# Splitting a weight conversion into four steps and moving a row sum by one iteration, in a fused attention and feed-forward kernel

## The chip, the cores and the metric

The kernel runs on one core of a Trainium2 chip. The metric is device time in microseconds (us), the median of three executions. The engines are named as the profile names them: PE (matmuls; its weight loads have a row of their own, PEld), DVE, ACT, POOL, and SP, which only issues DMAs here. Each engine works off its own instructions in order.

## The reference

Two blocks run one after the other. The first is a linear attention with decay over 4 batches, 8 heads, 768 positions and 48 channels per head. The state of each head is multiplied by `w` at every position and takes up the outer product of `k` and `v`; the position's own term is weighted by `u` instead:

```
cur = einsum('bhd,bhe->bhde', u * k_t, v_t)
y_t = einsum('bhd,bhde->bhe', r_t, state + cur)
state = w * state + einsum('bhd,bhe->bhde', k_t, v_t)
```

The second block takes the 3072 rows of 384 values, multiplies them by `w_in` (384 x 1024), computes `h * softmax(h)`, normalises each row to mean 0 and variance 1, scales the 1024 columns by `g_ln` and multiplies by `w_out` (1024 x 384). `w_in` and `w_out` arrive as 64-bit floats.

## The kernel before

The 3072 rows are 24 units of 128 rows (6 chunks of 4 batches). A loop over i from -2 on is a software pipeline written out by hand: in iteration i, unit i+4 is loaded, unit i+2 is transposed and gets its diagonal, unit i+1 gets its scores, unit i is finished (y and state), unit i-2 goes through the first matmul and the softmax, unit i-5 through the second matmul. The order in the program text is the order on each engine; nothing reorders it.

For a unit u the names are: `turn_r` (PE transposes `tr_ps`, DVE writes `rT`, L640), `decay_k` (POOL writes `kp`, L618), `turn_k` (PE `tk_ps`, ACT writes `kT`), `weigh_own` (two multiplications `rku` by POOL, or by DVE for units 0 to 2, L624 and L625; then DVE sums over the channels into `own`, L627), `diagonal` (8 ACT instructions write `AT`, L633, scaled by `own`), `scores` (PE `at`, DVE copies the upper triangle into `AT`, L661), `finish` (PE `y_ps` and `kv_ps`, ACT copies `xT`, DVE adds to `state`, L705 or L708, POOL decays it, L706), `ffn_in` (PE `h_ps`, L716; DVE row maximum `st`, L720; ACT `e`, L722), `unit` (DVE `solu`, L732; ACT square sum `sq`, L736; POOL `st`, L737 and L739), `normalise` (DVE, L744), `turn_ln` (PE `t_ps`, L754; DVE and ACT copy `lnT`, L756 and L758), `ffn_out` (PE `o_ps`, L765; ACT copies `o`, L768; SP stores it).

`h_ps` has one buffer: the first matmul of the next unit can't start before `solu` of this unit has read it. The pool `psM` has four buffers for `tr_ps`, `tk_ps`, the two halves of `t_ps`, `o_ps`, `y_ps` and `kv_ps`, taken in turn, so that the second half of `t_ps` takes the buffer of the last `kv_ps`.

The weights come in 14 pieces (0 to 5 of `w_in`, 128 x 512; 6 to 13 of `w_out`, 128 x 384), each loaded as raw words and converted in iterations -2 to 4 (1, 1, 2, 2, 3, 3, 2 pieces): ACT takes the magnitude (`mag`, L503); DVE clamps it, shifts it and puts the sign back (L504, L508, L510, writing `ma`); ACT scales the low word (`low`, L513); POOL adds both (L515 or L517); for `w_out` ACT scales the sum by `g_ln` (L518). All of a piece is emitted before the next piece:

```
for _ in range(conversions.get(i, 0)):
    convert(todo.pop(0))
    if ahead < len(pieces):
        load_weights(ahead)
        ahead += 1
```

Of the kernel before, what the change touches and what calls it, by code (L numbers as in the profile page):

```python
# [9 lines left out]
F32 = mybir.dt.float32  # L10
U32 = mybir.dt.uint32
ACT = mybir.ActivationFunctionType
ALU = mybir.AluOpType
AX = mybir.AxisListType
# [4 lines left out]
def general_path(  # L19
# [59 lines left out]
    def load(i):  # L79
        b, c = units[i]  # L80
        for t, src in ((kpads, k), (rpads, r), (vts, v)):
            nc.sync.dma_start(out=t[i % NLD][:, :, 0:D],
                              in_=src[b, :, ts(c, T), :].rearrange("h s d -> s h d"))
# [169 lines left out]
    def scores(i):  # L253
        X = live[i]
        AT = X["AT"] = ATs[i % NAT]
        A4 = AT.rearrange("p (a q) t -> p a q t", q=2)
        for ls in LEVELS:
            pss = [psA.tile([128, 2, HP, 64], F32, tag="at", name=f"at{q}") for q in range(2)]
            for n, L in enumerate(ls):
                lo, up = (X["kT"], X["rT"]) if L == 1 else (X["z"][L], X["z"][L])  # L260
                M = 64 if L == 64 else 128
                for a in range(HP):
                    for q in range(2):
                        rows = slice(q * P, q * P + D)
                        rhs = up[rows, a, :].rearrange("p (j o n) -> p j o n", o=2, n=L)[:, :, 1, :]
                        nc.tensor.matmul(pss[q][0:M, n, a, :], lo[rows, a, 0:M], rhs,
                                         start=True, stop=True)
            for n, L in enumerate(ls):
                for q in range(2):
                    dst = halves(A4[:, :, q, :], L)[1]  # L270
                    src = pss[q][:, n].rearrange("p a (j n) -> p a j n", n=L)
                    if L in masks:
                        m = masks[L].rearrange("p o (j n) -> p o j n", n=L)
                        nc.vector.copy_predicated(
                            dst, m.to_broadcast([128, HP, 64 // L, L]), src)
                    else:
                        for j in range(64 // L):
                            rows = slice(2 * L * j, 2 * L * j + L)
                            nc.scalar.copy(out=dst[rows, :, j, :], in_=src[rows, :, j, :])
# [89 lines left out]

    N = len(units)  # L370
    todo = list(range(len(pieces)))
    ahead = 6
    prepare(0)
    for i in range(N + LAG):
        j = i - LAG
        if i + 2 < N:
            load(i + 2)
        if i + 1 < N:
            prepare(i + 1)
# [6 lines left out]
        if j >= 0:  # L386
            ffn_in(j)
        if i < N:
            scores(i)
        if j >= 0:  # L390
            ffn_out(j)
        if i < N:
            finish(i)
# [3 lines left out]
def direct_path(  # L397
# [19 lines left out]
    nc = tc.nc  # L417
    B, H, S, D = r.shape
# [9 lines left out]
    LA, LO = 2, 3  # L428
# [5 lines left out]
    apool = ctx.enter_context(tc.tile_pool(name="apool", bufs=2))  # L434
    fpool = ctx.enter_context(tc.tile_pool(name="fpool", bufs=2))
    wpool = ctx.enter_context(tc.tile_pool(name="wpool", bufs=2))
# [17 lines left out]
    def load(i, which="krv"):  # L454
        b, c = units[i]
        for t, src, n in ((kpads, k, "k"), (rpads, r, "r"), (vts, v, "v")):
            if n in which:
                nc.sync.dma_start(out=t[i % len(t)][:, :, 0:D],
                                  in_=src[b, :, ts(c, T), :].rearrange("h s d -> s h d"))
# [4 lines left out]
    g_sb = const.tile([128, KF], F32, name="g_sb")  # L464
# [7 lines left out]
                        in_=u.rearrange("h d -> (h d)").partition_broadcast(128))  # L472
# [4 lines left out]
    def words(x):  # L477
# [5 lines left out]
    pieces = [(w_in_sb[:, c, ts(n, NX)], w_in_w[ts(c, 128), ts(n, 2 * NX)], None)  # L483
              for n in range(dff // NX) for c in range(KD)]
# [5 lines left out]
        raws[j] = wpool.tile([128, dst.shape[1], 2], U32, tag="raw", name="raw", bufs=5)  # L490
        nc.sync.dma_start(out=raws[j].rearrange("p n o -> p (n o)"), in_=src)

    def convert(j):
        dst, _, f = pieces[j]
        n = dst.shape[1]
        raw = raws.pop(j)
        lo, hi = raw[:, :, 0], raw[:, :, 1]
        mag = wpool.tile([128, n], F32, tag="mag", name="mag")
        ma = wpool.tile([128, n], U32, tag="ma", name="ma")
        low = wpool.tile([128, n], U32, tag="low", name="low")  # L500


        nc.scalar.activation(out=mag, in_=hi.bitcast(F32), func=ACT.Abs)  # L503
        nc.vector.tensor_scalar(out=mag, in0=mag, scalar1=FLOOR, scalar2=CEIL,  # L504
                                op0=ALU.max, op1=ALU.min)


        nc.vector.tensor_scalar(out=ma, in0=mag.bitcast(U32), scalar1=3, scalar2=0x3FFFFFF8,  # L508
                                op0=ALU.logical_shift_left, op1=ALU.bitwise_and)
        nc.vector.scalar_tensor_tensor(out=ma, in0=hi, scalar=0xC0000000, in1=ma,  # L510
                                       op0=ALU.bitwise_and, op1=ALU.bitwise_or)

        nc.scalar.activation(out=low, in_=lo, func=ACT.Copy, scale=2.0 ** -29)  # L513
        if f is None:
            nc.gpsimd.tensor_tensor(out=dst.bitcast(U32), in0=ma, in1=low, op=ALU.add)  # L515
        else:
            nc.gpsimd.tensor_tensor(out=ma, in0=ma, in1=low, op=ALU.add)  # L517
            nc.scalar.activation(out=dst, in_=ma.bitcast(F32), func=ACT.Copy,  # L518
                                 scale=g_sb[:, f : f + 1])

# [65 lines left out]
    def make_wt():  # L586

        nc.gpsimd.memset(wt, 0.0)
        for q in range(2):
            rows = slice(q * P, q * P + D)  # L590
            nc.gpsimd.tensor_copy(out=wt[rows, :, q, :],
                                  in_=pw[rows, 0, 7].unsqueeze(2).to_broadcast([D, HP, D]))
# [16 lines left out]
    live = {}  # L609
# [5 lines left out]
    def decay_k(i):  # L615
        X = live[i] = {}
        X["kp"] = apool.tile([128, H, P], F32, name="kp", bufs=4)
        nc.gpsimd.tensor_mul(X["kp"].rearrange("p h d -> p (h d)"),  # L618
                             kpads[i % NLD].rearrange("p h d -> p (h d)"),
                             kdec.rearrange("p a d -> p (a d)"))  # L620

    def weigh_own(i, engine):
        rku = apool.tile([128, H, D], F32, name="rku")
        engine.tensor_mul(rku, kpads[i % NLD][:, :, 0:D], u_bc)  # L624
        engine.tensor_mul(rku, rku, rpads[i % NLD][:, :, 0:D])  # L625
        own = live[i]["own"] = small.tile([128, H, 1], F32, name="own")
        nc.vector.tensor_reduce(out=own[:, :, 0], in_=rku, axis=AX.X, op=ALU.add)  # L627

    def diagonal(i):
        X = live[i]  # L630
# [4 lines left out]
    def turn_r(i):  # L635
        rT = live[i]["rT"] = apool.tile([128, HP, T], F32, name="rT", bufs=3)
        ps = psM.tile([128, HP, T], F32, tag="m", name="tr_ps")
        for a in range(HP):
            nc.tensor.transpose(ps[:, a, :], pair(rpads[i % NLD], a), ident)
        nc.vector.tensor_mul(rT, ps, fore)  # L640
# [129 lines left out]


    N = len(units)
    todo = list(range(len(pieces)))
    ahead = 5
    conversions = {-2: 1, -1: 1, 0: 2, 1: 2, 2: 3, 3: 3, 4: 2}
    decay_k(0)
    for i in range(-2, N + LA + LO):
        j, l = i - LA, i - LA - LO
        drain = i >= N + LA - 1
        if 0 <= i and i + 4 < N:  # L780
            load(i + 4)
        if i + 2 < N:
            turn_r(i + 2)
            if i <= 0:
                weigh_own(i + 2, nc.vector)
            turn_k(i + 2)
        if i + 3 < N:
            decay_k(i + 3)
        if i == -2:
            make_wt()  # L790
        for _ in range(conversions.get(i, 0)):
            convert(todo.pop(0))
            if ahead < len(pieces):
                load_weights(ahead)
                ahead += 1
        if i + 2 < N:
            diagonal(i + 2)
        if i == 0:
            nc.sync.dma_start(out=g_sb, in_=moe_g_ln.rearrange("(c p) -> p c", p=128))
        if i == 10:  # L800
            check_range()
        if 0 <= l and not (drain and i > N + LA - 1):
            turn_ln(l)
        if 0 <= j < N:
            ffn_in(j)
        if 0 <= i + 1 < N:
            scores(i + 1)
        if 0 <= j < N:
            unit(j)
        if 0 <= i and i + 3 < N:  # L810
            weigh_own(i + 3, nc.gpsimd)
        if drain and l + 1 < N:
            turn_ln(l + 1)
        if 0 <= l:
            ffn_out(l)
        if 0 <= j < N:
            normalise(j)
        if 0 <= i < N:
            finish(i)
# [43 lines left out]
```

## Time and profile before

| what | value |
|---|---|
| time, median of 3 | 455.01 us (453.76 to 455.08) |
| the profiled execution's own time | 454.42 us |
| its span, first to last instruction | 452.7 us |
| busy: PE, PEld | 399.3 us (88%), 248.9 us (55%) |
| busy: DVE, ACT, POOL | 207.5 us (46%), 183.2 us (40%), 125.4 us (28%) |
| mean granted PE clock | 0.946 |
| DMA moved in all | 25.92 MB, mean 57 GB/s |

The profile comes from one execution. Its own time is a little below the median of the runs. A share of busy time is a mean over the whole span, and the start of this kernel, in which weights are loaded and converted, differs from the rest; so the views are read stage by stage.

### The profile page before, as it was taken

The numbers are of one execution on the slowest core, as the hardware profiler recorded it, in microseconds if no ns is written. First come the engines' busy times: TensorE is split into PE (matmuls) and PEld (weight loads), VectorE is DVE, ScalarE is ACT, GpSimd is POOL, SyncE is SP. The second block draws the span as 40 slices with busy tenths as digits, with TensorE's granted clock in tenths as the row PEclk, the third lists the DMA queues.
The fourth block names the chain that finished last, engine by engine and source line by source line (L and its number), as shares of the span: only waits on it lengthen the run. The fifth ranks groups of instructions, "written<-read, shape, count | busy, mean of one in ns | idle before, by whom it ended". The sixth has DMA issues, their size and how long they took to land.

```text
span 452.7 us, 7184 instructions
## 1 busy us (share of the span) xinstructions
PE 399.3 (88%) x2853; PEld 248.9 (55%) x2853; DVE 207.5 (46%) x395; ACT 183.2 (40%) x422; POOL 125.4 (28%) x163
## 2 busy tenths in 40 slices
PE   2598081829999999999999999999999999999995
PEld 2485041325665665675665665666566565655563
DVE  6976454544435345454353443534525433523410
ACT  1872626264434434434343452443443443322320
POOL 4565141414421421421431342242142120000000
PEclk9879677677999999999999999999999999999999
DMA  9999660000303311330330330230330000000011
GB/s 183 261 237 159 152 91 17 1 0 1 71 20 52 70 43 29 70 63 9 70 71 1 70 72 15 57 71 19 52 71 19 0 19 20 19 1 17 17 38 41
DMA packets 81592, 25.92 MB, mean 57 GB/s; under 512 B 76557, under 2 KB 79758, under 8 KB 81550
## 3 DMA queue, kind: packets, MB, share of 16 engines
q1 hardware_dynamic: 81406, 25.18, 27.6%
q8 instruction: 24, 0.39, 0.4%
q10 hardware_dynamic: 144, 0.20, 0.1%
q14 instruction: 18, 0.15, 0.1%
HBM read 20.65 MB, written 4.72 MB: 56 GB/s over the span
## 4 chain that ended last, share of the span: by engine, by line
PE 46%; DVE 25%; POOL 12%; ACT 9%; issue 6%; DMA 1%; POOLq 0%; ACTq 0%; DVEq 0%
PE h_ps L716 24%; PE o_ps L765 13%; DVE solu L732 5%; PE t_ps L754 4%; ACT e L722 4%; POOL rku L625 4%; POOL rku L624 4%; DVE st L720 4%; DVE solu L744 3%; DVE own L627 2%; PE y_ps L686 2%; POOL st L739 2%; ACT sq L736 2%; POOL ma L517 2%; DVE ma L510 2%
## 5 line engine op out<-in xcount | busy, mean ns | idle before, releaser
L716 PE MATMUL h_ps<-w_in_sb,xT 128*128 128x512 f32 x288 | 134.5, 618 | 25.6 <-DVE solu L732 25.2
L765 PE MATMUL o_ps<-w_out_sb,lnT 128*128 128x384 f32 x384 | 129.5, 491 | 0.0
L716 PEld LDWEIGHTS h_ps<-w_in_sb,xT 128*128 128x128 f32 x288 | 55.3, 199 | 87.9 <-issue 86.7
L765 PEld LDWEIGHTS o_ps<-w_out_sb,lnT 128*128 128x128 f32 x384 | 71.2, 190 | 47.9 <-issue 1.0
L720 DVE TENSOR_REDUCE st<-h_ps 128x1 f32<-128x1024 f32 x24 | 29.4, 1224 | 92.0 <-PE h_ps L716 92.0
L737 POOL TENSOR_SCALAR st<-st 128x1 f32<-128x1 f32 x24 | 4.6, 190 | 233.3 <-ACT sq L736 233.3
L722 ACT ACTIVATE e<-h_ps,st 128x1024 f32<-128x1024 f32 x24 | 26.7, 1111 | 95.3 <-DVE st L720 95.3
L633 ACT ACTIVATE AT<-ident,own 128x128 f32<-128x128 f32 x192 | 58.7, 389 | 5.2 <-DVE own L627 5.2
L627 DVE TENSOR_REDUCE own<-rku 128x8 f32<-128x384 f32 x24 | 13.3, 553 | 86.8 <-POOL rku L625 86.6
L736 ACT ACTIVATE sq<-solu,st 128x1024 f32<-128x1024 f32 x24 | 27.6, 1149 | 47.8 <-DVE st L734 47.8
L754 PE MATMUL t_ps<-ident,solu 128*128 128x128 f32 x192 | 29.3, 284 | 9.5 <-ACT xT L698 8.1
L658 PEld LDWEIGHTS at<-rT,kT 48*128 48x128 f32 x384 | 25.7, 198 | 19.8 <-issue 19.0
L658 PE MATMUL at<-rT,kT 48*128 48x128 f32 x384 | 30.6, 298 | 2.7 <-DVE AT L661 2.6
L618 POOL TENSOR_TENSOR kp<-kpad,kdec 128x512 f32<-128x512 f32 x24 | 31.2, 1302 | 6.4 <-ACT kdec L568 5.3
L661 DVE COPY_PREDICATED AT<-later,at 128x512 f32<-128x512 uint32 x48 | 32.0, 722 | 0.0
L732 DVE SCALAR_TENSOR_TENSOR solu<-h_ps,st,e 128x1024 f32<-128x1024 f32 x24 | 30.8, 1284 | 0.8
L754 PEld LDWEIGHTS t_ps<-ident,solu 128*128 128x128 f32 x192 | 22.1, 145 | 15.3 <-ACT xT L698 8.3
L686 PE MATMUL y_ps<-AT,vt 128*32 128x128 f32 x768 | 26.3, 279 | 0.0
L744 DVE TENSOR_SCALAR solu<-solu,st 128x1024 f32<-128x1024 f32 x24 | 20.3, 845 | 10.8 <-POOL st L739 10.8
L648 ACT COPY kT<-tk_ps 128x512 f32<-128x512 f32 x24 | 14.0, 583 | 26.6 <-PE tk_ps L647 26.6
L706 POOL TENSOR_TENSOR state<-state,wt 128x384 f32<-128x384 f32 x16 | 16.0, 1002 | 29.7 <-DVE state L705 29.7
L702 PE MATMUL kv_ps<-vt,kp 128*128 128x96 f32 x160 | 23.5, 292 | 0.0
(67 smaller groups left out, 368.4 us busy)
## 6 DMA issues: line engine op xcount, KB each, us to landing
kpad<-in_k_dram SPq DMA_DIRECT2D x24, 192.0 KB, 3.4
rpad<-in_r_dram SPq DMA_DIRECT2D x24, 192.0 KB, 4.0
vt<-in_v_dram SPq DMA_DIRECT2D x24, 192.0 KB, 3.9
out_dram<-o SPq DMA_DIRECT2D x24, 192.0 KB, 2.0
raw<-in_moe_w_in_dram SPq DMA_DIRECT2D x6, 512.0 KB, 5.8
raw<-in_moe_w_out_dram SPq DMA_DIRECT2D x8, 384.0 KB, 3.4
u_bc<-in_u_dram ACTq DMA_DIRECT2D x1, 192.0 KB, 3.5
wq<-in_w_dram SPq DMA_DIRECT2D x1, 1.5 KB
```

The source lines that it names most:

```text
L633: nc.scalar.activation(out=AT[:, h, :], in_=ident, func=ACT.Copy, scale=X["own"][:, h])
L658: nc.tensor.matmul(pss[q][:, a, :], X["kT"][rows, a, :], X["rT"][rows, a, :], start=True, stop=True)
L661: nc.vector.copy_predicated(A4[:, :, q, :], later.to_broadcast([128, HP, T]), pss[q])
L686: nc.tensor.matmul(y_ps[32 * g : 32 * g + 32, j, :], lhsT, rhs, start=(g not in opened), stop=stop, skip_group_check=True)
L716: nc.tensor.matmul(h_ps[:, ts(n, NX)], X["xT"][:, j, :], w_in_sb[:, j, ts(n, NX)], start=(j == 0), stop=(j == KD - 1))
L720: nc.vector.tensor_reduce(out=nmax, in_=h_ps, axis=AX.X, op=ALU.max, negate=True)
L722: nc.scalar.activation(out=e, in_=h_ps, func=ACT.Exp, bias=nmax, accum_out=se)
L732: nc.vector.scalar_tensor_tensor(out=solu, in0=h_ps, scalar=rs, in1=e, op0=ALU.mult, op1=ALU.mult, accum_out=tot)
L736: nc.scalar.activation(out=sq, in_=solu, func=ACT.Square, bias=nmu, accum_out=ss)
L744: nc.vector.tensor_scalar(out=X["solu"], in0=X["solu"], scalar1=nmu, scalar2=rstd, op0=ALU.add, op1=ALU.mult)
L754: nc.tensor.transpose(t_ps[:, f, :], X["solu"][:, ts(4 * g + f, 128)], ident)
L765: nc.tensor.matmul(o_ps, X["lnT"][:, f, :], w_out_sb[:, f, :], start=(f == 0), stop=(f == KF - 1))
```

## The change

`convert` is cut into four steps. Step a holds both ACT readings of the raw words (`mag` and `low`), step b the three DVE instructions, step c the addition on POOL, step d the scaling by `g_ln` on ACT. In an iteration, a and b of all its pieces come first, then the diagonal, then `decay_k`, then c of all its pieces; d follows in the next iteration, ahead of that one's a. `mag` and `low` get three buffers and `ma` four (two each before). `weigh_own` is cut in two: the multiplications (`weigh`) for unit i+3 stand behind the c steps of iteration i, ahead of the POOL instructions of `unit`, and run on POOL for all units but the first; the sum (`sum_own`) stands one iteration later, behind `turn_r`. `decay_k` moves behind the diagonal, `make_wt` from iteration -2 to -1, and the load of `g_ln` ahead of the loads of unit 4. The diff without the renamed and unchanged lines:

```diff
-    def convert(j):
+    def convert_a(j):
         raw = raws.pop(j)
+        n = raw.shape[1]
         lo, hi = raw[:, :, 0], raw[:, :, 1]
+        mag = wpool.tile([128, n], F32, tag="mag", name="mag", bufs=3)
+        low = wpool.tile([128, n], U32, tag="low", name="low", bufs=3)
         nc.scalar.activation(out=mag, in_=hi.bitcast(F32), func=ACT.Abs)
+        nc.scalar.activation(out=low, in_=lo, func=ACT.Copy, scale=2.0 ** -29)
+        step[j] = hi, mag, low
+    def convert_b(j):
+        hi, mag, low = step[j]
+        ma = wpool.tile([128, mag.shape[1]], U32, tag="ma", name="ma", bufs=4)
...
+        step[j] = ma, low
+    def convert_c(j):
+        dst, _, f = pieces[j]
+        ma, low = step[j]
+        nc.gpsimd.tensor_tensor(out=dst.bitcast(U32) if f is None else ma, in0=ma, in1=low,
+                                op=ALU.add)
+    def convert_d(j):
+        dst, _, f = pieces[j]
+        ma, low = step.pop(j)
+        if f is not None:
             nc.scalar.activation(out=dst, in_=ma.bitcast(F32), func=ACT.Copy,
                                  scale=g_sb[:, f : f + 1])
-    def weigh_own(i, engine):
-        rku = apool.tile([128, H, D], F32, name="rku")
+    def weigh(i, engine):
+        rku = live[i]["rku"] = apool.tile([128, H, D], F32, name="rku")
         engine.tensor_mul(rku, kpads[i % NLD][:, :, 0:D], u_bc)
         engine.tensor_mul(rku, rku, rpads[i % NLD][:, :, 0:D])
+
+    def sum_own(i):
         own = live[i]["own"] = small.tile([128, H, 1], F32, name="own")
-        nc.vector.tensor_reduce(out=own[:, :, 0], in_=rku, axis=AX.X, op=ALU.add)
+        nc.vector.tensor_reduce(out=own[:, :, 0], in_=live[i]["rku"], axis=AX.X, op=ALU.add)
...
+        if i == 0:
+            nc.sync.dma_start(out=g_sb, in_=moe_g_ln.rearrange("(c p) -> p c", p=128))
         if 0 <= i and i + 4 < N:
             load(i + 4)
         if i + 2 < N:
             turn_r(i + 2)
-            if i <= 0:
-                weigh_own(i + 2, nc.vector)
+            if i == -2:
+                weigh(0, nc.vector)
+            sum_own(i + 2)
             turn_k(i + 2)
-        if i + 3 < N:
-            decay_k(i + 3)
-        if i == -2:
-            make_wt()
-        for _ in range(conversions.get(i, 0)):
-            convert(todo.pop(0))
+        for p in now:
+            convert_d(p)
+        now = [todo.pop(0) for _ in range(conversions.get(i, 0))]
+        for p in now:
+            convert_a(p)
+            convert_b(p)
             if ahead < len(pieces):
                 load_weights(ahead)
                 ahead += 1
         if i + 2 < N:
             diagonal(i + 2)
-        if i == 0:
-            nc.sync.dma_start(out=g_sb, in_=moe_g_ln.rearrange("(c p) -> p c", p=128))
+        if i + 3 < N:
+            decay_k(i + 3)
+        for p in now:
+            convert_c(p)
+        if i + 3 < N:
+            weigh(i + 3, nc.gpsimd)
+        if i == -1:
+            make_wt()
...
-        if 0 <= i and i + 3 < N:
-            weigh_own(i + 3, nc.gpsimd)
```

## Rows read from the trace of the kernel before

**Rows 1.** Page part 2: busy tenths of PE and DMA in 40 slices.
```profile
PE   2598081829999999999999999999999999999995
...
DMA  9999660000303311330330330230330000000011
```

**Rows 2.** Waits, whole span: engine, line, releaser; us in total, times, longest us.
```profile
PE h_ps L716 <- DVE solu L732: 25.2, 2, 14.1
...
ACT w_out_sb L518 <- POOL ma L517: 31.6, 8, 7.9
...
PE t_ps L754 <- ACT xT L698: 8.1, 1, 8.1
...
PEld t_ps L754 <- DVE state L705: 5.0, 15, 0.3
```

**Rows 3.** Timeline, 56 to 100 us: start, duration, engine, line, operands [idle before, releaser].
```profile
56.95 1.28 DVE L732 SCALAR_TENSOR_TENSOR solu<-h_ps,st,e 128x1024 f32<-128x1024 f32 x1
...
60.06 0.56 POOL L739 TENSOR_TENSOR st<-st,neg_half 128x1 f32<-128x1 f32 x1
...
60.44 0.55 ACT L503 ACTIVATE mag<-raw 128x384 f32<-128x384 f32 x1
...
63.16 1.27 DVE L744 TENSOR_SCALAR solu<-solu,st 128x1024 f32<-128x1024 f32 x1
...
65.42 0.34 DVE L504 TENSOR_SCALAR mag<-mag 128x384 f32<-128x384 f32 x1
...
70.51 0.99 POOL L517 TENSOR_TENSOR ma<-ma,low 128x384 uint32<-128x384 uint32 x1 [2.62 <-DVE ma L510]
71.54 0.61 ACT L518 ACTIVATE w_out_sb<-ma,g_sb 128x384 f32<-128x384 f32 x1 [2.08 <-POOL ma L517]
...
72.62 0.36 DVE L504 TENSOR_SCALAR mag<-mag 128x384 f32<-128x384 f32 x1 [2.25 <-ACT mag L503]
...
73.95 1.22 DVE L720 TENSOR_REDUCE st<-h_ps 128x1 f32<-128x1024 f32 x1
...
78.09 1.09 ACT L722 ACTIVATE e<-h_ps,st 128x1024 f32<-128x1024 f32 x1
...
79.69 1.28 DVE L732 SCALAR_TENSOR_TENSOR solu<-h_ps,st,e 128x1024 f32<-128x1024 f32 x1
...
81.13 8.10 PE L716 MATMUL h_ps<-w_in_sb,xT 128*128 128x512 f32 x12 [11.17 <-DVE solu L732]
...
98.75 1.28 DVE L732 SCALAR_TENSOR_TENSOR solu<-h_ps,st,e 128x1024 f32<-128x1024 f32 x1
```

**Rows 4.** Timeline: DVE's sum for unit 4.
```profile
41.16 0.55 DVE L627 TENSOR_REDUCE own<-rku 128x8 f32<-128x384 f32 x1 [2.20 <-POOL rku L625]
```

**Rows 5.** Groups by line: operation and count | busy us, mean ns | idle before.
```profile
L624 POOL TENSOR_TENSOR rku<-kpad,u_bc 128x384 f32<-128x384 f32 x21 | 21.2, 1009 | 0.0
```

**Rows 6.** Timeline: a DVE shift beside a POOL addition.
```profile
35.35 1.32 POOL L515 TENSOR_TENSOR w_in_sb<-ma,low 128x512 uint32<-128x512 uint32 x1 [2.09 <-DVE ma L510]
...
35.57 1.38 DVE L508 TENSOR_SCALAR ma<-mag 128x512 uint32<-128x512 uint32 x1
```

**Rows 7.** Timeline, 168 to 178 us: one iteration of the long even stretch.
```profile
168.54 0.55 DVE L627 TENSOR_REDUCE own<-rku 128x8 f32<-128x384 f32 x1 [4.34 <-POOL rku L625]
...
169.73 0.55 DVE L705 TENSOR_TENSOR state<-kv_ps,state 128x384 f32<-128x384 f32 x1
...
170.31 2.44 ACT L633 ACTIVATE AT<-ident,own 128x128 f32<-128x128 f32 x8
170.34 0.42 PEld L754 LDWEIGHTS t_ps<-ident,solu 128*128 128x128 f32 x4 [0.35 <-DVE state L705]
...
177.17 4.81 PEld L765 LDWEIGHTS o_ps<-w_out_sb,lnT 128*128 128x128 f32 x16
```

**Rows 8.** Windows: busy us of PE, PEld, DVE, ACT, POOL; PE clock; DMA share, GB/s.
```profile
39.00:41.00 2.00, 1.85 (x16) 1.09 (x18) 0.00 (x0) 0.00 (x0) 1.92 (x3) 1.00 0.94 262
102.00:107.00 5.00, 5.00 (x12) 3.09 (x13) 2.45 (x5) 2.28 (x8) 3.07 (x4) 0.50 0.00 0
```

More of the change, by code (lines that the diff above doesn't have):

```diff
@@ L491, in load_weights @@
         nc.sync.dma_start(out=raws[j].rearrange("p n o -> p (n o)"), in_=src)
-    def convert(j):
-        dst, _, f = pieces[j]
-        n = dst.shape[1]
+    step = {}
+    def convert_a(j):
         raw = raws.pop(j)
+        n = raw.shape[1]
         lo, hi = raw[:, :, 0], raw[:, :, 1]
-        mag = wpool.tile([128, n], F32, tag="mag", name="mag")
-        ma = wpool.tile([128, n], U32, tag="ma", name="ma")
-        low = wpool.tile([128, n], U32, tag="low", name="low")
+        mag = wpool.tile([128, n], F32, tag="mag", name="mag", bufs=3)
+        low = wpool.tile([128, n], U32, tag="low", name="low", bufs=3)
         nc.scalar.activation(out=mag, in_=hi.bitcast(F32), func=ACT.Abs)
+        nc.scalar.activation(out=low, in_=lo, func=ACT.Copy, scale=2.0 ** -29)
[3 more added lines that the diff above has]
+        ma = wpool.tile([128, mag.shape[1]], U32, tag="ma", name="ma", bufs=4)
         nc.vector.tensor_scalar(out=mag, in0=mag, scalar1=FLOOR, scalar2=CEIL,
@@ L511, in convert @@
                                        op0=ALU.bitwise_and, op1=ALU.bitwise_or)
[L513 to L517, printed above, removed]
+        step[j] = ma, low
[8 more added lines that the diff above has]
+        if f is not None:
             nc.scalar.activation(out=dst, in_=ma.bitcast(F32), func=ACT.Copy,
@@ L772, in direct_path @@
     N = len(units)
+    ahead = 5
     todo = list(range(len(pieces)))
-    ahead = 5
     conversions = {-2: 1, -1: 1, 0: 2, 1: 2, 2: 3, 3: 3, 4: 2}
+    now = []
     decay_k(0)
@@ L797, in direct_path @@
             diagonal(i + 2)
-        if i == 0:
-            nc.sync.dma_start(out=g_sb, in_=moe_g_ln.rearrange("(c p) -> p c", p=128))
+        if i + 3 < N:
[6 more added lines that the diff above has]
+            make_wt()
         if i == 10:
             check_range()
-        if 0 <= l and not (drain and i > N + LA - 1):
+        if 0 <= l and not i > N + LA - 1:
             turn_ln(l)
```

## The prediction

> **What bounds the kernel now.** I read the slices first. A slice is 452.7 / 40 = 11.3 us. PE is at 9 or more from the tenth slice to the last but one; before that it reads 2598081829 [rows 1]. So there are two stages: a start of some 102 us in which PE often stands still, and an even stretch that PE fills. A gain in the start has to shorten what PE waits for; one in the even stretch has to take away one of PE's own small waits.
>
> The list of waits names both. In the start, PE waited 25.2 us in two waits for `solu` (the one buffer of `h_ps`) and 8.1 us once for `xT`, which stands behind the softmax on ACT. ACT in turn waited 31.6 us for POOL's eight additions of the conversion [rows 2]. In the even stretch one wait is left: the second half of `t_ps` waits for the state addition, 15 times, 5.0 us in all [rows 2].
>
> The timeline of the start says why. For a piece of `w_out`, POOL adds at 70.51, ACT scales at 71.54, and only then ACT reads the next piece, so DVE's next clamp comes at 72.62 after 2.25 us of idling [rows 3]. All pieces go through this round trip, and the row maximum of the softmax (73.95) stands behind the last one on DVE. Behind it ACT still has the last scaling and the diagonal to do, so `e` starts at 78.09 and `solu` ends at 79.69 + 1.28 = 80.97. The three ends of `solu` for units 0, 1 and 2 are 58.23, 80.97 and 100.03 [rows 3]: periods of 22.74 us (three pieces) and 19.06 us (two). After the third comes `xT`, then `t_ps`, and from there PE runs through.
>
> **The change, part by part.**
>
> *Round trip and diagonal (iterations 3 and 4).* With a and b first, ACT never waits for POOL within an iteration; DVE's sets of three instructions follow each other. I count from the end of `solu`. POOL's `st` ends at 60.06 + 0.56 = 60.62, so 2.4 us after it. Before, `normalise` still had to wait for `rku` and `own`; now it follows at once. From its start to the first clamp of the next iteration took 65.42 - 63.16 = 2.26 us [rows 3], to which the moved sum adds 0.55 [rows 4]: the first set starts 5.25 us after `solu`. ACT is ready by then: its first magnitude started 60.44 - 58.23 = 2.2 us after `solu` and took 0.55; three scalings at 0.61 now stand ahead [rows 3], which makes 4.6 us.
>
> A set without POOL beside it takes 73.95 - 72.62 = 1.33 us [rows 3]. The next one now runs beside the addition of the one before it. A shift of 512 columns beside such an addition took 1.38 us, against an addition of 1.32 [rows 6]; for 384 columns the addition is 0.99 [rows 3], so 0.33 less: about 1.05 instead of 0.36, and 2.0 us for the set. Bounds: 1.33 (no clash) and 1.33 + 0.99 = 2.3 (all of the addition). I take 2.0, the value that the clashing row gives.
>
> The Trainium skill ("SBUF — State Buffer", section "Who interferes with whom") states that a DVE `tensor_scalar` on SBUF and a POOL instruction exclude each other for a whole instruction, since they share one pair of ports. That speaks against emitting b of one piece beside c of the last; by it a set costs the 2.0 us, without it 1.33, and the six sets with a neighbour would be 4 us cheaper together. The shift that lasted as long as the addition agrees [rows 6].
>
> Three sets: 1.33 + 2 x 2.0 = 5.3, so the last ends 10.6 us after `solu`. The first matmul, 8.1 us even at its slowest [rows 3], is done before. The diagonal (2.44 us, [rows 7]) is no longer between: ACT ends its readings 4.6 + 5 x 0.55 = 7.3 us after `solu` and the diagonal at 9.8. Then the row maximum 1.22 and a hand-over of 0.1, then from `e` to the end of `solu` 80.97 - 78.09 = 2.9 [rows 3]. Sum: 14.8 us instead of 22.74, 7.9 gained. With two pieces: 12.8 instead of 19.06, 6.3 gained.
>
> *Iterations -2 to 2.* POOL takes over four multiplications from DVE (units 1 and 2), about 1.0 us each [rows 5], and DVE's sums wait for them. On the other side `state` and `rT` no longer stand behind the sum. Bounds for when the sum for unit 4 runs: 4.0 us later (all four in the way) to 2.2 earlier (the wait that it has now, [rows 4]). It still stands behind the last addition of `w_in` and the same two multiplications, so I leave it at 41.16, the row nearest to both. Then the sets of pieces 6 to 8 start at 41.7, all three beside POOL work (`kp` first): 6.0 us, then 1.3 and 2.9 as above: `solu` of unit 0 ends at 51.9 instead of 58.23, 6.3 gained.
>
> The start is thus 6.3 + 7.9 + 6.3 = 20.5 us shorter, and `xT` and `t_ps` move by as much.
>
> *Loads.* `load_weights` waits, on SP, for the last DVE reading of the piece just converted, as before; behind it on SP stand the loads of the next unit. These now come earlier. DMA is near full for four slices and at 6 tenths for two [rows 1]: the same bytes at full rate are through after (4 + 1.2) x 11.3 = 59 us at the latest. The last two pieces are needed after `solu` of unit 1, at 51.9 + 14.8 = 66.7. Cost 0, with 2 us (59 against 51.9 + 5.25 = 57.2 for pieces 9 to 11) if they are late. The `g_ln` load is one more issue ahead of unit 4; `make_wt` and `decay_k` move on POOL alone, where 2.2 us of DVE waiting [rows 4] is the cover for the first and the bounds above hold for both.
>
> *Clock.* The gap of PE ahead of `t_ps` was 8.1 us [rows 2]. The last period shrinks by 6.3, PE's own work in it doesn't: 1.8 us stay. After the 8.1 us gap PE ran 5.0 us at a granted clock of 0.50 (1.2 GHz) [rows 8]; a stretch with only short gaps (1.85 busy of 2.00) kept 1.00 (2.4 GHz). Bounds: 0 and half of 5.0. I take 2.5, since 1.8 us is nearer to the second row.
>
> *The even stretch.* The state addition (169.73) stands behind `normalise`, that behind the sum (168.54), which waited 4.34 us for POOL's `rku` [rows 7]. With `rku` ahead of POOL's `st` and the sum gone to the next iteration, `normalise` runs before `kv_ps` is there, and the addition follows `kv_ps` at once. All 15 waits go: 5.0 us. Late next: the sum now stands behind `rT`, so the diagonal (170.31) starts up to 1.2 us later, `lnT` behind it on ACT ends at about 170.31 + 1.2 + 2.44 + 0.6 = 174.5; `o_ps` needs it at 177.17 [rows 7]. Margin 2.6 us, no cost. `rku` now runs beside `rT`, the sum and `lnT` on DVE; bounds 0 and 2.0 us per iteration within that same margin.
>
> *Sum.* 454.42 - 20.5 - 5.0 - 2.5 = 426.4 for an execution like the profiled one. That one was 0.59 below the median of 455.01, so 427.0.
>
> **The rivals.**
>
> A. Another wait takes the place of the state addition, for instance `y_ps`'s or `o_ps`'s buffer in the same turn of four. For: PE's slack is only 0.35 us there [rows 7]. Against: no other PE wait is listed in the even stretch. Price 5.0: 432.0.
>
> B. The sums for units 1 and 2, now at DVE's head behind POOL's new work, delay everything by the upper bound of 4.0, and the gap ahead of `t_ps` still drops the clock: 427.0 + 4.0 + 2.5 = 433.5. For: DVE already waits 2.20 us there [rows 4]. Against: POOL is idle for 2 us and more before its additions [rows 6].
>
> C. No clash between sets and additions: 4.0 less, 423.0. Against it stands the row of 1.38 us [rows 6].
>
> D. Slower: the sum at DVE's head finds `rku` not ready in each iteration of the even stretch. Then `rT` is done but the diagonal, `lnT` and with it `o_ps` are late, one for one, in about 17 iterations. To eat 28 us it must cost 1.65 us in each, which with the margin of 2.6 means a sum 4.3 us later than I place it. Nothing puts `rku` there: its loads are issued an iteration ahead, and POOL is idle for most of an iteration.
>
> E. It doesn't do what it says: ACT or DVE stays blocked by buffers (`low` has three, so piece p waits for the addition of piece p - 3), the start shrinks by half: 427.0 + 10 + 2.5 = 439.5. Against: those additions are an iteration old.
>
> **How the numbers follow.** Forecast 0.58 (421 to 431 with its bounds), A 0.11, B 0.12, C 0.08, E 0.05, D 0.04, no change 0.02. About 0.3%, 1.4 us, is what a measurement of this kernel tells from none. Faster by more than that: all but D and no change, 0.94; within 0.02; slower 0.04. The range takes in the forecast, A, B and C: 420.5 to 435.5.
>
> **What would show it.** Right: ends of `solu` for units 0 to 2 near 52, 67 and 79.5; ACT's waits for POOL's additions gone; shifts of about 1.05 us among the sets; `t_ps` near 81.5 with full clock soon after; no `t_ps` wait for `state`, and iterations 0.35 us shorter in the even stretch. Wrong: `solu` ends later than 60 for unit 0, a new PE wait repeated in each iteration, or a DVE wait for `rku` at the sum beyond iteration 2.

## The result, and the profile after

The changed kernel takes 429.59 us (median of four runs, 428.08 to 429.73); the kernel before took 454.94 us beside it (453.76 to 455.08). The ratio is 0.944, with a 95% interval of 0.9415 to 0.9467. The forecast was 427.0 us with a range of 420.5 to 435.5, so the time is 2.6 us above the forecast and inside the range. The profiled run took 429.58 us with a span of 427.9 us, against 454.42 and 452.7 before: 24.8 us less span. PE is busy 395.9 us (93%), before 399.3 (88%).

The page of the kernel after, its slices (40 of 10.7 us, in tenths), answers [rows 1]:

```profile
PE   2579397799999999999999999999999999999995
...
DMA  8999891003303303303213213123120000000011
```

PE reads 9 from the ninth slice on, some 86 us into the span, where before it did so from the tenth, at some 102 us. DMA, which moves the same bytes, reads 8 or 9 for six slices in a row, before 9 for four and 6 for two.

The waits of the kernel after (engine, line, releaser; us in total, times, longest) answer [rows 2]:

```profile
DVE state L722 <- PE kv_ps L719: 24.9, 15, 1.7
...
PE h_ps L733 <- DVE solu L749: 9.0, 2, 6.5
DVE own L644 <- POOL rku L640: 7.0, 4, 2.9
...
PE t_ps L771 <- ACT xT L715: 3.1, 1, 3.1
```

PE's two waits for `solu` went from 25.2 to 9.0 us and the one for `xT` from 8.1 to 3.1. ACT's wait for the additions of `w_out` (31.6 us) and PE's 15 waits for `state` (5.0 us) are no longer listed: in their place DVE's state addition waits 15 times for `kv_ps`, and between 105 and 420 us the list names no wait of PE for another engine. DVE's sum waits for POOL four times, the last at 42.30 us, and then no more.

The timeline of the kernel after (start, duration, engine, line, operands, idle before and its releaser) answers [rows 3] and [rows 4]:

```profile
42.22 1.27 POOL L633 TENSOR_TENSOR kp<-kpad,kdec 128x512 f32<-128x512 f32 x1
...
42.30 0.55 DVE L644 TENSOR_REDUCE own<-rku 128x8 f32<-128x384 f32 x1 [1.19 <-POOL rku L640]
42.77 0.94 DVE L512 TENSOR_SCALAR mag<-mag 128x384 f32<-128x384 f32 x1
...
51.40 1.28 DVE L749 SCALAR_TENSOR_TENSOR solu<-h_ps,st,e 128x1024 f32<-128x1024 f32 x1
...
55.05 1.27 POOL L633 TENSOR_TENSOR kp<-kpad,kdec 128x512 f32<-128x512 f32 x1
...
55.12 1.75 DVE L761 TENSOR_SCALAR solu<-solu,st 128x1024 f32<-128x1024 f32 x1 [2.23 <-POOL st L756]
...
58.31 0.34 DVE L512 TENSOR_SCALAR mag<-mag 128x384 f32<-128x384 f32 x1
...
58.69 0.36 DVE L516 TENSOR_SCALAR ma<-mag 128x384 uint32<-128x384 uint32 x1
...
59.79 1.00 POOL L526 TENSOR_TENSOR ma<-ma,low 128x384 uint32<-128x384 uint32 x1 [3.47 <-DVE ma L518]
...
59.95 1.05 DVE L516 TENSOR_SCALAR ma<-mag 128x384 uint32<-128x384 uint32 x1
...
66.34 1.28 DVE L749 SCALAR_TENSOR_TENSOR solu<-h_ps,st,e 128x1024 f32<-128x1024 f32 x1
...
79.39 1.28 DVE L749 SCALAR_TENSOR_TENSOR solu<-h_ps,st,e 128x1024 f32<-128x1024 f32 x1
```

`solu` of units 0, 1 and 2 ends at 52.68, 67.62 and 80.67 (start plus 1.28): periods of 14.94 us (three pieces) and 13.05 us (two), before 22.74 and 19.06. Of DVE's shifts for pieces 9 to 11, the second (59.95) takes 1.05 us beside POOL's addition, the first (58.69), with none beside it, 0.36. The first clamp in the iteration before (42.77) takes 0.94 us beside `kp`, against 0.34 (58.31).

PE's rows of the timeline where the start ends, in the kernel before:

```profile
101.98 1.97 PE L754 MATMUL t_ps<-ident,solu 128*128 128x128 f32 x8 [8.06 <-ACT xT L698]
103.74 6.98 PE L716 MATMUL h_ps<-w_in_sb,xT 128*128 128x512 f32 x12
110.65 1.16 PE L658 MATMUL at<-rT,kT 48*128 48x128 f32 x16
```

The same rows in the kernel after, with the first matmul of the period that ends there:

```profile
67.78 7.08 PE L733 MATMUL h_ps<-w_in_sb,xT 128*128 128x512 f32 x12 [2.48 <-DVE solu L749]
...
82.62 1.82 PE L771 MATMUL t_ps<-ident,solu 128*128 128x128 f32 x8 [3.07 <-ACT xT L715]
84.23 6.31 PE L733 MATMUL h_ps<-w_in_sb,xT 128*128 128x512 f32 x12
90.48 1.16 PE L675 MATMUL at<-rT,kT 48*128 48x128 f32 x16
```

Windows of the kernel after (columns as in [rows 8]) show PE's clock there, 0.50 in the second:

```profile
82.60:84.00 1.40, 1.38 (x7) 1.38 (x8) 0.85 (x2) 1.40 (x3) 0.52 (x1) 0.58 0.00 0
84.00:86.00 2.00, 2.00 (x6) 0.96 (x5) 2.00 (x4) 0.55 (x3) 1.49 (x2) 0.50 0.00 0
```

These rows divide the 24.8 us. Up to the first `t_ps`: 101.98 - 82.62 = 19.36 (forecast 20.5). From there to `at` behind the next `h_ps`: 8.67 us before, 7.86 after, so 0.81 from the clock (forecast 2.5). The rest of the span: 452.7 - 110.65 = 342.05 against 427.9 - 90.48 = 337.42, so 4.63 (forecast 5.0).

### The profile page after: what moved, and what is told of

It reads as the page before. It is cut to its first block, busy times and chain, and to the rows that moved or that the text cites. A ratio compares the mean times of both kernels' runs of the same rounds, so it can differ in the third digit from the quotient of the medians.

```text
span 427.9 us, 7198 instructions
## 1 busy us (share of the span) xinstructions
PE 395.9 (93%) x2853; PEld 249.7 (58%) x2853; DVE 212.4 (50%) x391; ACT 185.0 (43%) x422; POOL 128.7 (30%) x167
## 4 chain that ended last, share of the span: by engine, by line
PE 80%; DVE 13%; POOL 2%; issue 2%; ACT 1%; DMA 1%; POOLq 0%; ACTq 0%; DVEq 0%
PE o_ps L782 30%; PE h_ps L733 26%; PE y_ps L703 7%; PE t_ps L771 5%; PE at L675 5%; PE kv_ps L719 4%; DVE ma L516 3%; DVE ma L518 2%; PE tr_ps L656 2%; PE tk_ps L664 2%; DVE mag L512 1%; DVE tab L567 1%; POOL rku L639 1%; POOL rku L640 1%; DVE solu L749 1%
## 5 line engine op out<-in xcount | busy, mean ns | idle before, releaser
L761 DVE TENSOR_SCALAR solu<-solu,st 128x1024 f32<-128x1024 f32 x24 | 21.4, 892 | 54.2 <-POOL st L756 54.2
L771 PE MATMUL t_ps<-ident,solu 128*128 128x128 f32 x192 | 25.8, 279 | 3.1 <-ACT xT L715 3.1
L640 POOL TENSOR_TENSOR rku<-rku,rpad 128x384 f32<-128x384 f32 x23 | 23.0, 999 | 1.8
```

Of the source, the lines that this page charges most:

```text
L771: nc.tensor.transpose(t_ps[:, f, :], X["solu"][:, ts(4 * g + f, 128)], ident)
```

## The experiments

All times are medians of four runs; the kernel before had medians of 454.48 to 454.98 us beside them.

**1. The four steps alone.** The sums and their multiplications stay where they were (for units 1 and 2 on DVE), and so does `make_wt`; `decay_k` stands behind the diagonal, as in the change:

```diff
-            sum_own(i + 2)
+            if i <= 0:
+                weigh_own(i + 2, nc.vector)
...
+        if 0 <= i and i + 3 < N:
+            weigh_own(i + 3, nc.gpsimd)
```

> Only the four steps of the conversion; multiplications and sum of a unit stay together behind the POOL instructions of the softmax, as before. Theory (two separate gains: the round trip in the start, the sum in front of the state addition in the even stretch): the even stretch keeps its 15 waits of t_ps for the state addition, +4.6 us against the changed kernel, and in the start the first DVE set follows solu after 7.2 us instead of 5.6, +1.6 in each of two periods: 429.6 + 4.6 + 3.2 = 437.4 us. Rival (the steps alone carry everything, the sum is only tidied up): 430 us, and no t_ps waits for the state.

Measured: 437.41 us (436.91 to 438.31), ratio 0.9623 (0.9596 to 0.9649). From its waits, and from its timeline behind `solu` of unit 0:

```profile
PEld t_ps L769 <- DVE state L720: 5.0, 15, 0.3
```

```profile
56.59 1.27 POOL L633 TENSOR_TENSOR kp<-kpad,kdec 128x512 f32<-128x512 f32 x1
...
56.66 0.55 DVE L642 TENSOR_REDUCE own<-rku 128x8 f32<-128x384 f32 x1 [4.27 <-POOL rku L640]
57.13 1.28 DVE L759 TENSOR_SCALAR solu<-solu,st 128x1024 f32<-128x1024 f32 x1
```

The 15 waits of PE for the state addition are back, 5.0 us as in [rows 2]; experiment 2, which moves `rku` and the sum alone, has none. So moving them is what removes the waits. The `solu` periods are 16.54 and 14.64 us, 1.6 longer than after: DVE's wait ahead of `normalise` is 4.27 us for `rku` instead of 2.23 for `st`, and `normalise` itself takes 1.28 us instead of 1.75. That the median meets the expectation to a hundredth is in part luck: in the profiled run `t_ps` comes 2.70 us later than after, where I had 3.2, and from there to `at` it takes 9.02 us against 7.86, which I had not counted.

**2. The moved sum alone.** a to d of a piece follow each other again, and `decay_k` stands ahead of them, as before the change:

```diff
-        for p in now:
-            convert_d(p)
-        now = [todo.pop(0) for _ in range(conversions.get(i, 0))]
-        for p in now:
+        if i + 3 < N:
+            decay_k(i + 3)
+        for _ in range(conversions.get(i, 0)):
+            p = todo.pop(0)
             convert_a(p)
             convert_b(p)
+            convert_c(p)
+            convert_d(p)
...
-        if i + 3 < N:
-            decay_k(i + 3)
-        for p in now:
-            convert_c(p)
```

> Only the sum one iteration later with its multiplications ahead of the softmax's POOL instructions; each piece is converted whole before the next, as before. Theory: the round trip ACT - DVE - POOL - ACT of about 3.6 us per piece and the diagonal behind it stay; the first clamp comes some 1.9 us earlier in each of three periods, and the even stretch loses its 15 waits (4.6 us): 454.9 - 5.7 - 4.6 = 444.6 us. Rival (the start is bound by DVE's work, not by the round trip): 433 us or less.

Measured: 447.47 us (446.52 to 447.85), ratio 0.9851 (0.9824 to 0.9877): 2.9 us above what I expected. The direction held (no wait of PE for `state`; ACT's wait for POOL's additions still there, 26.2 us), the size did not:

```profile
42.51 0.55 DVE L644 TENSOR_REDUCE own<-rku 128x8 f32<-128x384 f32 x1 [1.18 <-POOL rku L640]
...
61.40 1.27 POOL L633 TENSOR_TENSOR kp<-kpad,kdec 128x512 f32<-128x512 f32 x1
61.47 1.75 DVE L761 TENSOR_SCALAR solu<-solu,st 128x1024 f32<-128x1024 f32 x1 [2.23 <-POOL st L756]
```

The sum for unit 4 is 1.35 us later than in [rows 4], and `solu` of unit 0 ends at 59.04, 0.81 later than before. I had the first clamp, and so `solu`, 1.9 us earlier in each of three periods: the first period alone is thus 2.7 us worse than expected. The other two are 21.09 and 17.55 us, 1.65 and 1.51 shorter than before, together 0.6 less than expected; `normalise` takes 1.75 us in them beside `kp`, where the row of before has 1.27 [rows 3]. In the profiled run the stretch behind `t_ps` gave 1.0 us back (7.67 against 8.67). The two halves give 17.1 and 7.0 us alone, 24.1 together, against 25.3 of the whole: their gains nearly add up.

**3. No additions for `w_out`.** Step c is left out for the eight pieces of `w_out`, whose low words are then missing:

```diff
     def convert_c(j):
         dst, _, f = pieces[j]
         ma, low = step[j]
+        if f is not None:
+            return
```

> The changed kernel without POOL's eight additions for w_out; this leaves out the low words of w_out. Theory (DVE's sets are what the start waits for, and each is lengthened by the addition beside it): the shift takes 0.36 us instead of 1.05 in five sets, so solu of unit 2 ends 3.4 us earlier: 426.2 us. Rival (the sets have slack, first matmul or diagonal ends last): 429.6 us, unchanged, though the shifts get shorter.

Measured: 427.68 us (426.94 to 428.69), ratio 0.9419 (0.9388 to 0.9451), so 1.9 us less than the whole change, where I expected 3.4. DVE and POOL in the iteration of pieces 6 to 8:

```profile
42.97 0.94 DVE L512 TENSOR_SCALAR mag<-mag 128x384 f32<-128x384 f32 x1
...
43.66 1.13 POOL L640 TENSOR_TENSOR rku<-kpad,u_bc 128x384 f32<-128x384 f32 x1
43.95 1.05 DVE L516 TENSOR_SCALAR ma<-mag 128x384 uint32<-128x384 uint32 x1
44.86 1.00 POOL L641 TENSOR_TENSOR rku<-rku,rpad 128x384 f32<-128x384 f32 x1
45.03 1.24 DVE L518 SCALAR_TENSOR_TENSOR ma<-raw,ma 128x384 uint32<-128x384 uint32 x1
...
46.58 0.36 DVE L516 TENSOR_SCALAR ma<-mag 128x384 uint32<-128x384 uint32 x1
```

Here no addition stands beside any set, and the later shifts take 0.36 us again: the 1.05 us is the clash with POOL. But nothing holds POOL up any more, so `rku` moves forward and meets the first set, whose shift and sign take 1.05 and 1.24 us now (the clamp takes 0.94 beside `kp`, as after). Taking away one POOL instruction let the next one into its place, and `solu` of unit 0 came no earlier (52.87). The iterations that follow are 1.0 and 0.32 us shorter (13.94 and 12.73), so that `t_ps` comes 1.13 us earlier in the profiled run (81.49). That run took 426.98 us, 2.6 less than the one after; the larger part, 1.63 us, lies behind `t_ps`, where PE ran at full clock (6.23 us from `t_ps` to `at` against 7.86). The median's 1.9 us are therefore not the worth of the additions alone.

**4. PE kept busy ahead of `t_ps`, first try.** 24 extra transposes of unit 7's `kp` into its own `tk_ps`, which doesn't change what is computed:

```diff
     def turn_k(i):
...
-        for a in range(HP):
+        for a in list(range(HP)) * (7 if i == 7 else 1):
```

> The changed kernel with the four transposes of kp for unit 7 made seven times over, 24 more, about 2.6 us of PE work at full clock in the gap of 3.07 us ahead of the first t_ps. Theory (the gap lets the granted clock fall, and the first matmul behind it runs partly at 0.50): t_ps and the first matmul of that iteration run at 1.00, 1.75 us gained: 427.9 us. Rival (the clock falls for another reason, or the work is too light to hold it): 429.6 us with the same 0.50 after 82.6 us; if the transposes delay t_ps, up to 431.

Measured: 431.31 us (429.71 to 431.49), ratio 0.9482 (0.945 to 0.9514): a miss, on the wrong side. PE:

```profile
79.04 3.22 PE L664 MATMUL tk_ps<-ident,kp 128*128 128x128 f32 x28
82.83 0.66 PE L771 MATMUL t_ps<-ident,solu 128*128 128x128 f32 x4 [0.57 <-ACT xT L715]
84.69 1.06 PE L771 MATMUL t_ps<-ident,solu 128*128 128x128 f32 x4 [1.21 <-DVE state L722]
85.54 6.64 PE L733 MATMUL h_ps<-w_in_sb,xT 128*128 128x512 f32 x12
```

The gap closed to 0.57 us and the first half of `t_ps` ran at full clock. The second half then waited 1.21 us for the state addition, a wait that the changed kernel doesn't have, and the clock fell behind that. In the built program the second half had been given another buffer of `psM`, the one whose reader is that addition; in the changed kernel the second half does not wait for it, since `t_ps` ends at 84.44 and the addition at 84.43. So the experiment had a second edit in it that I had not meant, and says nothing on a gap that is only filled.

**5. The same with 16 transposes**, which leave the buffers as they were (5 in place of 7 in the diff above).

> The changed kernel with 16 more transposes of kp for unit 7, some 1.8 us of PE work in the gap of 3.07 us ahead of the first t_ps; with this number the second half of t_ps keeps the buffer that it has in the changed kernel (with 24 more it took that of kv_ps, and waited 1.2 us for the state addition). Theory (the gap lets the clock fall): the first matmul behind it runs at 1.00, 1.7 us gained, 427.9 us. Rival (the clock is not set by that gap alone; one fill run had its fall behind a gap of 1.4 us, and another kernel none behind 3.0): 429.6 us, with runs at either clock.

Measured: 428.38 us (428.28 to 428.59), ratio 0.9428 (0.9412 to 0.9443): 1.2 us below the whole change, 0.5 above what I expected, and its four runs lie within 0.31 us where those of the change spread over 1.65.

```profile
80.05 2.35 PE L664 MATMUL tk_ps<-ident,kp 128*128 128x128 f32 x20
82.86 1.14 PE L771 MATMUL t_ps<-ident,solu 128*128 128x128 f32 x8 [0.47 <-ACT xT L715]
83.84 5.32 PE L733 MATMUL h_ps<-w_in_sb,xT 128*128 128x512 f32 x12
89.08 1.16 PE L675 MATMUL at<-rT,kT 48*128 48x128 f32 x16
```

From `t_ps` to `at` it takes 89.08 - 82.86 = 6.22 us: that is what the stretch costs at full clock. Of the 8.67 us before, 2.45 were thus to be had, which is the 2.5 of the forecast; the profiled run after got 0.81 of it. Unlike in the fourth experiment, the gap was filled and no new one opened. The rival's 429.6 us did not come, though the mean clocks of the four runs do differ (0.966 to 0.988).

**6. `kp` out of the way of `normalise`.** From iteration 2 on (unit 5), POOL multiplies `kp` behind `rku`, ahead of its wait for `st`; until unit 4 it stays where the change has it (the `live` line only keeps a place for the unit's tiles):

```diff
         if i + 3 < N:
+            live[i + 3] = {}
+        if i < 2 and i + 3 < N:
             decay_k(i + 3)
         for p in now:
             convert_c(p)
         if i + 3 < N:
             weigh(i + 3, nc.gpsimd)
+        if i >= 2 and i + 3 < N:
+            decay_k(i + 3)
```

> The changed kernel with kp on POOL behind the additions and rku from iteration 2 on, instead of ahead of them. Theory (normalise on DVE stands still beside POOL's kp, 1.75 us instead of 0.81, and the first set of iteration 2 beside kp takes 0.6 us more; both are on the path of the start): two times 0.95 and 0.6 us gained, 427.1 us. Rival (normalise has slack in the start): 429.6 us; or kp now meets another DVE instruction and nothing is gained.

Measured: 426.20 us (425.98 to 426.23), ratio 0.9377 (0.9361 to 0.9392): 3.4 us below the whole change, 0.9 better than I expected.

```profile
51.64 1.26 POOL L633 TENSOR_TENSOR kp<-kpad,kdec 128x512 f32<-128x512 f32 x1
...
55.02 0.81 DVE L761 TENSOR_SCALAR solu<-solu,st 128x1024 f32<-128x1024 f32 x1 [2.23 <-POOL st L756]
...
80.65 1.14 PE L771 MATMUL t_ps<-ident,solu 128*128 128x128 f32 x8 [0.89 <-ACT xT L715]
...
81.62 5.32 PE L733 MATMUL h_ps<-w_in_sb,xT 128*128 128x512 f32 x12
```

`normalise` takes 0.81 us instead of 1.75, twice in the start; `t_ps` comes 1.97 us earlier. PE now waits for `kp` ahead of `tk_ps`, so that less of its idle time lies in one piece ahead of `t_ps`, and `h_ps` runs at full clock: from `t_ps` to `at` it takes 6.22 us against 7.86. That second gain I had not expected. The 0.6 us of the first set came too (its clamp takes 0.35 us), but the sum for unit 4 was 0.5 us later (42.81), so `solu` of unit 0 ends only 0.09 earlier.

**7. DVE's own multiplications for units 1 and 2**, as before the change:

```diff
-            if i == -2:
-                weigh(0, nc.vector)
+            if i <= 0:
+                weigh(i + 2, nc.vector)
...
-        if i + 3 < N:
+        if 0 <= i and i + 3 < N:
             weigh(i + 3, nc.gpsimd)
```

> The changed kernel with the multiplications for units 1 and 2 on DVE, as before. Theory (the sum for unit 4 ran at 42.30 instead of 41.16 us since POOL's four new multiplications stand ahead of its additions): it runs at 41.2 again and everything behind it 1.1 us earlier, 428.5 us. Rival (DVE's multiplications beside POOL's work cost as much as POOL's do; the lateness is chance): 429.6 us or more.

Measured: 427.82 us (426.87 to 430.05), ratio 0.9428 (0.9395 to 0.9461). The median is 1.8 us below that of the change, but the runs overlap, so the time alone does not settle it. The profile does:

```profile
41.43 0.55 DVE L644 TENSOR_REDUCE own<-rku 128x8 f32<-128x384 f32 x1 [1.19 <-POOL rku L640]
```

The sum for unit 4 is back to 0.27 us from [rows 4]. In the eight profiles with POOL's multiplications for units 1 and 2 it runs at 42.30 to 42.81, in the five with DVE's, the kernel before among them, at 41.16 to 41.48. And `solu` of units 0 to 2 ends 0.87, 0.86 and 0.86 us earlier (51.81, 66.76, 79.81). POOL's four new multiplications cost 0.87 us in the start.

**8. The pieces spread over more iterations**, so that none has three; step d of the last two pieces stands in iteration 5 itself, ahead of the second matmul:

```diff
-    conversions = {-2: 1, -1: 1, 0: 2, 1: 2, 2: 3, 3: 3, 4: 2}
+    conversions = {-2: 1, -1: 1, 0: 2, 1: 2, 2: 2, 3: 2, 4: 2, 5: 2}
...
+        if i == 5:
+            for p in now:
+                convert_d(p)
+            now = []
```

> The changed kernel with the w_out pieces spread 2, 2, 2, 2 over iterations 2 to 5 instead of 3, 3, 2; the scaling of the last two stands in iteration 5 itself, ahead of the second matmul. Theory (in the start a period is the sum of DVE's sets and the softmax chain, 1.95 us for each further set): two periods lose one set each, solu of units 0 and 1 end 1.95 and 3.9 us earlier, 425.7 us; in iteration 5 DVE has room beside PE. Rival (the work is only moved: the second matmul of iteration 5 waits for its last weights): 429 us.

Measured: 426.33 us (425.81 to 426.97), ratio 0.938 (0.9363 to 0.9397), 0.6 above what I expected. `solu` of units 0 and 1 ends 1.69 and 3.65 us earlier (50.99, 63.97), where I had 1.95 and 3.9. The last two pieces no longer stand before the third `solu`, and their sets then run where PE has work of its own.

**9 to 11. Versions from these.** Spread pieces and `kp` behind `rku` together; the same with DVE's multiplications for units 1 and 2; and the latter with 16 extra transposes of `r` for unit 7. The move of `kp` is that of experiment 6, from iteration 2 on, and not "until unit 4" as the first expectation has it.

> Edit: the pieces spread 1, 1, 2, 2, 2, 2, 2, 2 over the iterations and, until unit 4, the k times decay product of POOL behind the two rku multiplications. Theory (both effects are separate terms): spreading alone gave 426.33 and the move of kp alone 426.20, so 3.3 and 3.4 us below the changed kernel's 429.59; together 422.9, between 421.9 and 424.0, with solu of units 0 to 2 ending near 51, 63.3 and 75.5. Rival 1 (both gains come from the clock, each escaping or shortening the same slow h_ps): no more than the better of the two, 425.5 to 426.5. Rival 2 (the gap ahead of t_ps opens, since PE has less work to do in each period): h_ps at half clock, 424.5 to 425.5.

> Edit: as the kernel with spread pieces and kp behind rku, and DVE does the rku multiplications of units 1 and 2 itself, as before the change. Theory (POOL's four multiplications hold up the sum for unit 4 by 0.9 us, a term of its own): 422.0, 0.9 below the kernel without this edit, sum for unit 4 near 41.4. Rival (with kp out of the way POOL's rku is early enough and DVE's own four multiplications only lengthen its queue): equal to or up to 1.5 us above the kernel without this edit.

> Edit: as the kernel with spread pieces, kp behind rku and DVE's own rku multiplications for units 1 and 2; and PE repeats the four transposes of r for unit 7 five times, 16 more, into the same buffer, in the gap ahead of t_ps (some 1.1 us of work at full clock in an idle time of 2.49 us). Theory (the scatter of that kernel, 422.3 to 424.77, comes from the clock behind the gap ahead of t_ps): all runs near the best of that kernel, 421.8 to 422.8, at a clock of 0.98 or more. Rival 1 (the scatter has its cause elsewhere, such as the earlier gap of 5 us in the first iteration): median 423.9 as without the fill, with runs from 422 to 425. Rival 2 (the fill stands in the way of rT, which DVE takes up 2 us later): up to 1.1 us more, 425.0.

| kernel | median, us | runs, us | ratio to before, 95% |
|---|---|---|---|
| spread, `kp` | 424.77 | 421.82 to 426.16 | 0.933 to 0.9371 |
| and DVE's multiplications | 423.87 | 422.30 to 424.77 | 0.9309 to 0.9345 |
| and the fill | 421.63 | 420.93 to 421.90 | 0.9245 to 0.9278 |

The first came 1.9 us above what adding the two gains gave, outside of the stretch that I had named, though its fastest run (421.82) is below it. The median lies where the second rival had it (424.5 to 425.5, a gap ahead of `t_ps` and `h_ps` at half clock), but the one run with a trace is the fastest, with `h_ps` at 5.32 us and `solu` of units 0 to 2 at 50.37, 62.42 and 74.52, as early as the theory asked for. So neither is decided for the other runs. The second differs from the first by less than either scatters; its sum for unit 4 is 1.15 us earlier (41.40 against 42.55), but whether the time gains is not settled. The third is the best version of all, 8.0 us below the change, and all of its runs are faster than every run without the fill: they lie within 0.97 us instead of 2.47, as the theory for it had it, and the first rival (a median of 423.9, unchanged) falls. What the other runs without the fill lost, and where, no trace shows. The one that has a trace, the fastest (422.30), had a longer wait for `kp` just ahead of `t_ps`, and a granted clock of 0.54 from 76 to 78 us:

```profile
74.23 0.98 PE L664 MATMUL tk_ps<-ident,kp 128*128 128x128 f32 x4 [2.49 <-POOL kp L633]
75.79 1.97 PE L771 MATMUL t_ps<-ident,solu 128*128 128x128 f32 x8 [0.58 <-ACT xT L715]
```

With the fill:

```profile
71.58 2.35 PE L656 MATMUL tr_ps<-ident,rpad 128*128 128x128 f32 x20
...
76.44 1.14 PE L771 MATMUL t_ps<-ident,solu 128*128 128x128 f32 x8 [0.91 <-ACT xT L715]
77.42 5.32 PE L733 MATMUL h_ps<-w_in_sb,xT 128*128 128x512 f32 x12
```

The wait for `kp` is 0.95 us there, and from `t_ps` to `at` it takes 6.23 us against 7.15.

## Why the prediction was right, step by step

**Round trip and diagonal.** Right: 14.94 and 13.05 us against a forecast of 14.8 and 12.8. Experiment 1 shows that the four steps alone are worth most of it (16.54 and 14.64), and experiment 3 that the shift of 1.05 us, taken from a clashing row of another width [rows 6], is a clash with POOL. Rival C (no clash) falls, and so does E (the start shrinks by half only). What I left out is that `normalise` gets more of `kp` beside it: 1.75 us where I had kept 1.27 [rows 3], so that the first set starts 5.63 us after `solu` instead of 5.25. The 1.27 held a part of this clash already. In the kernel before, `kp` was on when `normalise` started at 63.16:

```profile
62.61 1.26 POOL L618 TENSOR_TENSOR kp<-kpad,kdec 128x512 f32<-128x512 f32 x1
```

After, `rku` stands ahead of POOL's `st`, so `kp` follows `st` at once and starts together with `normalise`. This comes from the move of `rku` and not from that of `decay_k`: experiment 1, which moves `decay_k` and leaves `rku`, has 1.28 us, experiment 2, which moves `rku` and leaves `decay_k`, has 1.75. The Trainium skill ("SBUF — State Buffer", section "Who interferes with whom") has the rule that I applied to the shift alone: it names `tensor_scalar` among the instructions that can contend with GpSimd for a port pair, and `normalise` is one too. The trace agrees in this case, 1.75 us beside `kp` and 0.81 without (experiment 6). I weighed the rule for the instructions that the change adds, and not for one that stood still while its neighbour moved.

**Iterations -2 to 2.** The term was 6.3 us and measured 58.23 - 52.68 = 5.55. The sum for unit 4 did not stay at 41.16 but came at 42.30, 1.1 us later; the three sets behind it took 5.76 us (42.77 to 48.53) where I had 6.0, which gave a part back. Its wait for POOL is shorter than before (1.19 against 2.20), but POOL itself is late, since units 1 and 2 are now multiplied there. Experiment 7, which gives them back to DVE, has it at 41.43. My bounds (2.2 earlier to 4.0 later) held it; rival B, which took the upper one, falls.

**Loads.** The cost of 0 was right: no wait for a piece's load is listed, and the sets of pieces 9 to 11 begin at 58.31, straight behind the sum. The moment was not: DMA still reads 9 in the slice that ends at 64 us, where I had its work done after 59.

**Clock.** The term that was most off: 0.81 us measured in the profiled run, 2.5 forecast. The size of the whole gain was right (2.45, experiment 5), the condition for it was not. I had the gap ahead of `t_ps` at 8.1 - 6.3 = 1.8 us; it is 3.07. The period shrank by 6.01, a little less than forecast, and PE's own work in it shrank as well: `h_ps` took 7.08 us instead of the 8.10 of [rows 3], since less of it ran at the lower clock: before, the granted clock was 0.50 from its start at 81.13 on, after it was 1.00 until 69.00. 8.06 - 6.01 + 1.02 = 3.07. "PE's own work in it doesn't" was the sentence that failed. Behind the 3.07 us gap PE ran at 0.50, 1.2 GHz, until about 86 us. Experiment 7, whose gap of 1.76 us is nearly the one that I had worked out, ran at full clock in its profiled run.

**The even stretch.** Right: 4.63 us against 5.0, all 15 waits gone and none in their place. Experiments 1 and 2 tie them to `rku` and the sum. Rivals A (another PE wait) and D (the sum late in every iteration) fall: after the start DVE's sum waits for nothing.

**The whole.** The sum had 28.0 us to come off the profiled execution, 24.8 came off its span. Of the 3.2 us between, 1.7 is the clock (2.5 - 0.81), 1.1 the start (20.5 - 19.36), 0.4 the even stretch. The forecast had 0.59 us added for the median, so it ended 2.6 us too low.

## What to carry to other kernels

When an instruction is moved, check what it will stand beside at its new place, and check the instructions that stay as well: in this case the longer `normalise` (1.75 us for 0.81) cost the start as much as a clash in the new work. A conversion that bounces between three engines gained most here when it was emitted step by step, each engine through all its pieces, with a step that nobody waits for one iteration later. A gap of PE that shrinks is not yet a clock that stays up: work out the gap with PE's own time at the new clock. A fill of work that is thrown away took 1.2 and 2.2 us off here, and lost 1.7 where it moved a buffer. And before a gain is credited to an edit, look at what the clock did in the same run: in experiments 3, 6 and 7 some 1.6 us of the profiled run's gain lay behind `t_ps`.

## What was not expected of the hardware

**The length of a gap does not say which clock follows.** Ahead of `t_ps`, gaps of 0.47, 0.89 and 1.76 us (experiments 5, 6 and 7) left the first `h_ps` behind it at 5.32 us, full clock; gaps of 3.07, 3.79, 4.78 and 6.59 us (after, experiments 1, 8 and 2) made it slower, up to 7.33. Between them the length does not decide alone: experiment 3 had a gap of 3.02 us and 5.32, experiment 4 two of 0.57 and 1.21 and 6.64, experiment 10 one of 0.58 behind a wait of 2.49 for `kp`, and 1.97 for `t_ps` in place of 1.14. What does decide stays open.

**The mean granted clock of a run does not rank the times.** The changed kernel took 428.08 us in one run, at a mean of 0.988, and 429.58 to 429.73 in three others at 0.963 to 0.968; that this run had its `t_ps` and `h_ps` at full clock fits the size (1.5 us, against 1.64 between 7.86 and 6.22), but it has no trace. In experiment 5 the means go from 0.966 to 0.988 and the times differ by 0.31 us only: in the profiled run, at 0.966, `h_ps` of the period before took 7.93 us (68.02), and still ended, at 75.95, ahead of DVE's row maximum (76.75), which its sets held up. In experiment 4 the fastest run has the lowest mean (429.71 us at 0.967, the others 431.29 to 431.49 at 0.984). So in these runs it mattered which matmul met the low clock, and a run's mean does not tell that.

**Four of DVE's instructions took longer beside POOL's multiplications and additions, one did not.** The clamp takes 0.94 us instead of 0.34, the shift 1.05 instead of 0.36, the merge of the sign 1.24 instead of 0.56 (experiment 3), `normalise` 1.75 instead of 0.81 (experiment 6). The sum `own` took 0.55 us beside `kp` (42.30 in the kernel after) and 0.54 without.

**A matter of the program, not of the chip:** in this kernel the buffers of `psM` are not simply taken in turn, as I had described them. Eight more transposes (24 in place of 16) gave the second half of `t_ps` another buffer and PE a wait of 1.21 us (experiments 4 and 5).
